# Pooled attention and a gated product: two batches' keys and values summed over eight by TensorE, conversions put behind the first product, and two more slots between a query's low part and its scores

## The chip, the cores and the metric

The kernel runs on one core of one Trainium2 chip. Its engines are TensorE (PE in the profile, with its weight loads as PEld), VectorE (DVE), ScalarE (ACT), GpSimd (POOL) and SyncE (SP), which here only starts DMAs. The metric is the device time of one execution in microseconds, as the median of several runs. The time before is 1088.79 us (three runs, 1088.64 to 1090.27).

## The reference

Queries, keys and values are [8 batches, 8 heads, 576 rows, 64]. Keys and values are averaged over groups of eight rows, so each head has 72 of them. Attention over these gives x with 4608 rows of 512. Then come two products with 1536 columns, their elementwise product, and a product back to 512 columns.

```python
k_p = k.reshape(B, H, Sp, pool, D).mean(axis=3)
v_p = v.reshape(B, H, Sp, pool, D).mean(axis=3)
scores = scale * np.matmul(q, k_p.transpose(0, 1, 3, 2))
scores = scores - np.max(scores, axis=-1, keepdims=True)
attn = np.exp(scores)
attn = attn / (np.sum(attn, axis=-1, keepdims=True) + 1e-09)
return np.matmul(attn, v_p).astype(np.float32)
...
a = x @ w_a
b = x @ w_b
return (a * b @ w_out).astype(np.float32)
```

The weights come from the host as 64-bit floating numbers (seen as pairs of 32-bit words), so the kernel has to convert them.

## The kernel before

**Precision.** Every matmul operand is split into a high part (a cast to float32r, by ScalarE) and a low part (the rest, a subtraction in the helper `low_part`, line 182, by VectorE or GpSimd). A product is then three matmuls: high by high, high by low and low by high. The names tell the part: `xh` and `xl`, `jha` and `jla` (weight a), `hh` and `hl` (gated product), `qh` and `ql` (queries).

**Tiles.** The 4608 rows make nine tiles of 512. A tile's products run over twelve column blocks f. `ffn_in(t, f)` makes `psa` and `psb` with 24 matmuls of 512 columns, and `gated` (line 551) multiplies them on VectorE. `ffn_out(t, f)` adds to four accumulators `acc` with 12 matmuls. A hand-written order takes tile 0 first. From block `LAG` = 4 on, tile 1 runs beside it, its gated product kept in DRAM and fetched later. From tile 2 on each tile runs alone.

**Attention.** The queries are cut into chunks of 128 or 64 rows; the first four (`early`) are all of tile 0 and belong to batch 0. Tile 1 takes the last 64 rows of batch 0 and most of batch 1. A chunk goes through `qh` (ScalarE), `ql` (GpSimd for the first four, else VectorE), scores on TensorE into `psc`, the maximum and its subtraction (lines 398 and 399 while i < `SUMMED`, else also a sum of two halves on line 434), the exponential, its sum and reciprocal, a multiplication (line 454), the split of the probabilities, transposes `ptr` (line 499), and per block of chunks the product with the values `po` (lines 532 to 535), whose parts are `xh` and `xl`. A tile's first product is issued only once the work of all its chunks has been (`have`, line 628).

**Keys and values.** `load_keys(b)` loads the four pairs of heads with 64 + 64 channels on the partitions. VectorE sums over eight (line 278). ScalarE and VectorE then write the high and low part to `kdiag`, which is block-diagonal over the two heads of a pair. `load_values(b)` does the same for `vdiag`. The values come from the host transposed, so that eight rows to be summed lie side by side. The last 8 of a head's 72 rows come from an extra array `vr`, three copies of them, and end in `vrem`. For batch 0 the raw data wait in parts of the weight buffers that aren't filled yet (`early_k` in `wb_raw`, `early_v` in `wo_raw`), and three of the four pairs of the values are summed by GpSimd in three additions (line 328). The two buffers of `kdiag` and `vdiag` alternate between batches.

**Weights.** `convert_weights(name, j, first)` goes through the twelve blocks of a, b and o. For each there are two ScalarE operations on the words (lines 222 and 223), three VectorE operations (224, 228 and 233) and the load of the next block's words. A block f + 1 is converted once product f - 1 of tile 0 has begun (`AHEAD` = 2, `begun`), so blocks 0 and 1 wait for no product. `split_weight` then makes the high and low parts for a product; the low part is on VectorE for a and b in the first twelve and on GpSimd otherwise.

**Order.** All engines' instructions are issued in an order that the class `Chains` works out at build time. Each piece of work is a generator. `yield n` lets n slots pass, `yield PE` queues for TensorE's turn, `wait` polls for marks, and ranks order what is due in one slot. `ffn_in` has four slots (one after every six wide matmuls), `ffn_out` two. Each engine then runs its instructions strictly in that order, held only by semaphores. Ahead of the first product `need` steps the chains until tile 0's x and the first parts of a and b are there. From tile 2 on, a chunk is started at `begin_at`, `CHUNK` = 32 slots ahead of its share of the previous tile's time, and loads of keys `KEYS_AHEAD` = 18 slots before that. After `ql`, `PROBS_GAP` = 2 slots pass before the scores; the same constant stands behind the probabilities. PSUM has one bank each for `psa` and `psb`, two for `att` (scores, transposes, `po`) and four for `acc`, which the first four chunks' scores borrow before the first product needs them.

Of the kernel before, what the change touches and what calls it, by code (L numbers as in the profile page):

```python
# [20 lines left out]
P = 128  # L21
# [27 lines left out]

SLOTS = 6  # L50
# [20 lines left out]
PROBS_GAP, VALUE_GAP = 2, 4  # L71
CHUNK = 32
# [4 lines left out]
EARLY_GAP, VALUES_START, KEYS_START, WEIGHTS_START, CONVERT_AFTER = 1, 2, 8, 10, 5  # L77


class Chains:  # L80
# [9 lines left out]
    def mark(self, *what):  # L90
        self.done.add(what)
# [30 lines left out]
def attn_moe_kernel(ctx: ExitStack, tc: tile.TileContext, q, k, v, vr, wa, wb, wo, out):  # L122
# [23 lines left out]
    mask = const.tile([P, 4], F32, name="mask")  # L146

# [38 lines left out]
    early_k = raw["b"].rearrange("p f c -> p (f c)")[:, NF * 512 - NK * S:].rearrange("p (g s) -> p g s", g=NK)  # L186
    early_v = raw["o"][:, NF - NK:, :]
    early_vr = raw["o"][:, NF - NK - NG:NF - NK, :]
# [5 lines left out]

    def load_early():
        load_raw_queries(0, early_q[:, 0])
        for g in range(NK):
            nc.sync.dma_start(early_k[:, g, :], k[0, :, g, :])
        load_raw_queries(1, early_q[:, 1])
        for g in range(0, NK, 2):  # L200
            nc.sync.dma_start(early_v[:, g:g + 2, :], v[0, :, g:g + 2, :])
        nc.sync.dma_start(early_vr[:NR], vr[0])
        for i in range(2, early):
            load_raw_queries(i, early_q[:, i])

    def convert_weights(name, j, first):
# [8 lines left out]
        yield first  # L215
        for f in range(NF):
            words = area[name].rearrange("p (c w) -> p c w", w=2)
# [19 lines left out]
            while f + 1 >= AHEAD and (len(begun) <= f + 1 - AHEAD or chains.now < begun[f + 1 - AHEAD] + 2 * j):  # L237
                yield 1
# [23 lines left out]

    def load_keys(b):
        kd = kdiag[b % 2]
        kp = tmp(f"kp_{b}")[:, :NK * SP].rearrange("p (g s) -> p g s", g=NK)
        for g0 in range(0, NK, 2):
            gs = slice(g0, g0 + 2)
            if b == 0:
                kraw = [early_k[:, g, :] for g in (g0, g0 + 1)]
            else:  # L270
                if g0:
                    yield from wait(("kraw", b, 0))
                kraw = [sb.tile([P, S], F32, tag="kv", name=f"kraw_{b}_{g}") for g in (g0, g0 + 1)]
                for j in range(2):
                    nc.sync.dma_start(kraw[j], k[b, :, g0 + j, :])
                yield 4
            for j in range(2):
# [6 lines left out]
                if b:  # L284
                    yield 1
            mark("kraw", b, g0)
            for e in range(2):
                r = slice(e * D, e * D + D)
                nc.scalar.mul(kd[r, gs, 0, e, :], kp[r, gs], 1.0 / POOL)
            if b:  # L290
                yield 1
            for e in range(2):
                r = slice(e * D, e * D + D)
                nc.vector.scalar_tensor_tensor(
                    out=kd[r, gs, 1, e, :],
                    in0=kp[r, gs],
                    scalar=1.0 / POOL,
                    in1=kd[r, gs, 0, e, :].bitcast(F32),
                    op0=ALU.mult,
                    op1=ALU.subtract,  # L300
                )
            mark("keys", b, g0)

    def load_values(b):
        vd = vdiag[b % 2]
        vrem = sb.tile([P, NG, 2, 2, D], F32R, tag="vrem", name=f"vrem_{b}")
        yield from wait(("keys", b, 2), ("values", b - 1))
        vp = sb.tile([P, NK + NG, D], F32, tag="vp", name=f"vp_{b}", bufs=1)
        for x0 in range(0, NK + NG, 2):
            if b == 0:  # L310
                vraw = [early_v[:, x, :] if x < NK else early_vr[:, x - NK, :] for x in (x0, x0 + 1)]
            else:
                if x0:
                    yield from wait(("vraw", b, x0 - 2))
# [463 lines left out]
```

## Time and profile before

| what | us |
|---|---|
| median of three runs | 1088.79 |
| the profiled execution | 1089.11 |
| its span | 1087.3 |
| outside the span | 1.8 |
| TensorE busy in the span | 1035.1 |
| VectorE busy | 589.7 |
| ScalarE busy | 515.3 |
| GpSimd busy | 513.0 |
| first product's first matmul starts | 70.19 |

The span runs from the first to the last instruction of the core. Busy times are sums over instructions. Those of TensorE are modelled at their ends, because matmuls overlap. A row of the timeline gives start, length, engine, line, operation, output and inputs, and in square brackets how long the engine stood idle before it and what released it. A row of the groups ends with busy time, mean length in nanoseconds, and idle time before. The mean granted TensorE clock of this execution is 0.993.

### The profile page before, as it was taken

To read this page: it belongs to the slowest core of one execution; us is meant where nothing else is said; L and a number is where in the kernel's file an instruction comes from. 1 tells how busy PE (TensorE), PEld (TensorE's weight loads), DVE (VectorE), ACT (ScalarE), POOL (GpSimd) and SP (SyncE) were. 2 spreads that over 40 slices of the span, in tenths; PEclk is the share of its full clock that TensorE was granted. 3 is DMA by queue.
4 is the path that set the end of the run, shared out by engine and by line. 5 is a ranking of instruction groups with operands and counts; after the bars stand their busy time and mean duration, and the time that the engine had idled before them with its cause. 6 is when DMAs were issued, how large, how long until landed. Compare 5 with 4: busy or idle time off the path is not lost.

```text
span 1087.3 us, 13572 instructions
## 1 busy us (share of the span) xinstructions
PE 1035.1 (95%) x4964; PEld 859.6 (79%) x4964; DVE 589.7 (54%) x941; ACT 515.3 (47%) x1035; POOL 513.0 (47%) x425
## 2 busy tenths in 40 slices
PE   4479999999999999999999999999998999999998
PEld 4367787888878888888877888888886888888886
DVE  8879967854675347534684346643567344322112
ACT  4656644454553454544553454444543454443332
POOL 6132200055565555555555555555554455554442
PEclk9999999999999999999999999999998999999999
DMA  6434445221330004000220002100220010001001
GB/s 219 117 129 135 141 136 174 93 94 46 114 109 1 1 23 127 26 1 1 95 90 1 1 19 90 45 1 1 93 83 0 1 59 1 1 1 39 1 1 39
DMA packets 32178, 63.79 MB, mean 59 GB/s; under 512 B 7376, under 2 KB 7376, under 8 KB 32112
## 3 DMA queue, kind: packets, MB, share of 16 engines
q1 hardware_dynamic: 32112, 62.93, 17.9%
q8 instruction: 39, 0.64, 0.2%
q14 instruction: 27, 0.22, 0.1%
HBM read 51.38 MB, written 11.53 MB: 58 GB/s over the span
## 4 chain that ended last, share of the span: by engine, by line
PE 84%; DVE 11%; ACT 2%; DMA 1%; issue 1%; SPq 0%; POOL 0%; DVEq 0%; ACTq 0%
PE psa L594 9%; PE psb L594 9%; PE acc L616 9%; PE psa L595 8%; PE psa L596 8%; PE acc L618 8%; PE acc L617 8%; PE psb L596 8%; PE psb L595 8%; PE ptr L499 2%; PE psc L428 2%; DVE ql L182 1%; DVE s L399 1%; PE psc L431 1%; PE po L534 1%
## 5 line engine op out<-in xcount | busy, mean ns | idle before, releaser
L551 DVE TENSOR_TENSOR h<-psb,h 128x512 f32<-128x512 f32 x108 | 74.5, 689 | 339.1 <-PE psb L596 335.0
L182 POOL TENSOR_TENSOR jlb<-wb_raw,jhb 128x512 fp32r<-128x512 f32 x88 | 114.5, 1301 | 264.1 <-ACT jhb L258 264.1
L182 POOL TENSOR_TENSOR jlo<-wo_raw,jho 128x512 fp32r<-128x512 f32 x108 | 144.0, 1334 | 116.5 <-ACT jho L258 116.5
L601 ACT COPY h<-psa 128x512 f32<-128x512 f32 x108 | 63.5, 588 | 268.6 <-PE psa L596 253.1
L594 PE MATMUL psa<-xh,jha 128*128 128x512 f32 x432 | 175.2, 406 | 0.0
L594 PE MATMUL psb<-xh,jhb 128*128 128x512 f32 x432 | 171.7, 398 | 0.6 <-DVE h L551 0.6
L616 PE MATMUL acc<-jho,hh 128*128 128x512 f32 x432 | 171.6, 397 | 0.0
L595 PE MATMUL psa<-xl,jha 128*128 128x512 f32 x432 | 170.8, 395 | 0.7 <-DVE xl L182 0.7
L596 PE MATMUL psa<-xh,jla 128*128 128x512 f32 x432 | 170.6, 395 | 0.0
L618 PE MATMUL acc<-jho,hl 128*128 128x512 f32 x432 | 168.6, 390 | 0.0
L596 PE MATMUL psb<-xh,jlb 128*128 128x512 f32 x432 | 168.6, 390 | 0.0
L595 PE MATMUL psb<-xl,jhb 128*128 128x512 f32 x432 | 168.5, 390 | 0.0
L617 PE MATMUL acc<-jlo,hh 128*128 128x512 f32 x432 | 168.3, 389 | 0.0
L182 POOL TENSOR_TENSOR jla<-wa_raw,jha 128x512 fp32r<-128x512 f32 x88 | 126.6, 1438 | 68.0 <-ACT jha L258 64.0
L564 ACT CAST hh<-h 128x512 fp32r<-128x512 f32 x100 | 62.2, 622 | 91.4 <-DVE h L551 86.7
L182 DVE TENSOR_TENSOR hl<-h,hh 128x512 fp32r<-128x512 f32 x100 | 90.2, 902 | 24.2 <-ACT hh L564 23.9
L596 PEld LDWEIGHTS psa<-xh,jla 128*128 128x128 f32 x432 | 82.6, 191 | 18.1
L595 PEld LDWEIGHTS psa<-xl,jha 128*128 128x128 f32 x432 | 82.8, 192 | 15.6 <-DVE xl L182 1.1
L618 PEld LDWEIGHTS acc<-jho,hl 128*128 128x128 f32 x432 | 81.1, 188 | 17.5
L596 PEld LDWEIGHTS psb<-xh,jlb 128*128 128x128 f32 x432 | 81.1, 188 | 17.4
L594 PEld LDWEIGHTS psa<-xh,jha 128*128 128x128 f32 x432 | 82.6, 191 | 15.0
L594 PEld LDWEIGHTS psb<-xh,jhb 128*128 128x128 f32 x432 | 81.2, 188 | 16.1 <-DVE h L551 1.0
(93 smaller groups left out, 1704.6 us busy)
## 6 DMA issues: line engine op xcount, KB each, us to landing
out<-y SPq DMA_DIRECT2D x36, 256.0 KB, 2.1
kraw<-in_k SPq DMA_DIRECT2D x28, 288.0 KB, 3.3
qraw<-in_q SPq DMA_DIRECT2D x28, 256.0 KB, 3.7
vraw<-in_v SPq DMA_DIRECT2D x28, 256.0 KB, 3.0
words<-in_wa SPq DMA_DIRECT2D x12, 512.0 KB, 3.5
words<-in_wb SPq DMA_DIRECT2D x12, 512.0 KB, 3.5
words<-in_wo SPq DMA_DIRECT2D x12, 512.0 KB, 3.6
vraw<-in_vr SPq DMA_DIRECT2D x14, 192.0 KB, 2.8
```

The costliest lines, as they stand in the source:

```text
L182: eng.tensor_tensor(out=lo, in0=src, in1=hi.bitcast(F32), op=ALU.subtract)
L428: nc.tensor.matmul(pt[:n, :2 * hk], qh[:, g, :n], kd[:, g].rearrange("p w e s -> p (w e s)"), start=True, stop=False)
L499: nc.tensor.transpose(ptr[:rows, g, :n], src, ident[:n, :n])
L551: nc.vector.tensor_tensor(out=h, in0=pt, in1=h, op=ALU.mult)
L564: nc.scalar.copy(hh, h)
L594: nc.tensor.matmul(pt, wh[:, c], xh[:, kk], start=(kk == 0), stop=False)
L595: nc.tensor.matmul(pt, wh[:, c], xl[:, kk], start=False, stop=False)
L596: nc.tensor.matmul(pt, wl[:, c], xh[:, kk], start=False, stop=(kk == NK - 1))
L601: nc.scalar.copy(h, pt)
L616: nc.tensor.matmul(acc[c], hh[:, cs], wh, start=first, stop=False)
L617: nc.tensor.matmul(acc[c], hh[:, cs], wl, start=False, stop=False)
L618: nc.tensor.matmul(acc[c], hl[:, cs], wh, start=False, stop=last)
```

## The change

Four things are done.

1. Keys and values of batches 0 and 1 come from the host in plain rows (`kn`, `vn`: 576 rows of 512 columns) and are loaded by `load_rows`, 128 rows to a partition block and 64 in the last, into unused parts of the weight buffers. TensorE sums over eight: `pool_keys` multiplies each block of the rows with `pool16`, a 128 x 16 matrix with a one where row and group agree, and gets keys already transposed; `pool_values` uses `place` and `remain`, which put each sum at its partition, in five matmuls that accumulate in `acc` banks. The splits, now in `split_keys` and `split_values`, read PSUM for these batches and SBUF for the others. The matmuls are in plain float32. `load_keys` and `load_values` stay for batches 2 to 7. The ranks and start slots of these chains change (`SPLITS` for batch 0, the rank behind the first four chunks for batch 1).
2. In `convert_weights` block 1 of a and b waits for the first product to begin, and o waits for the values of batch 1, whose raw data lie in its buffer, and for the first product. a's block 3 waits for the keys of batch 1.
3. `QUERY_GAP` = 4 slots stand between `ql` and the scores from tile 2 on (it was 2), and `CHUNK` is 34 (it was 32), so the scores keep their slot and `qraw`, `qh` and `ql` move ahead by two. Keys and values are tied to `begin_at` and move with it.
4. From tile 2 on a chunk's transposes wait until all weights are converted, since the transposed probabilities take the words' buffer.

```diff
+NB = -(-S // P)
+BY_PE = 2
...
-PROBS_GAP, VALUE_GAP = 2, 4
-CHUNK = 32
+QUERY_GAP, PROBS_GAP, VALUE_GAP = 4, 2, 4
+CHUNK = 34
...
+    pool16 = const.tile([P, P // POOL], F32, name="pool16")
+    words = raw["o"].rearrange("p f c -> p (f c)")
+    place = words[:, :NK * (P + P // POOL)].rearrange("p (k c) -> p k c", k=NK)
+    remain = words[:, 1024 - NR:1024]
...
+    early_k = [waiting("b", NF - NB), waiting("a", NF - early - NB)]
+    early_v = [waiting("o", NF - NB), waiting("o", NF - 2 * NB)]
...
+    def load_rows(dst, src):
+        whole = S // P
+        nc.sync.dma_start(dst[:, :whole], src[:whole * P].rearrange("(k p) c -> p k c", p=P))
+        nc.sync.dma_start(dst[:S - whole * P, whole], src[whole * P:])
...
     def load_early():
         load_raw_queries(0, early_q[:, 0])
-        for g in range(NK):
-            nc.sync.dma_start(early_k[:, g, :], k[0, :, g, :])
+        load_rows(early_k[0], kn[0])
         load_raw_queries(1, early_q[:, 1])
-        for g in range(0, NK, 2):
-            nc.sync.dma_start(early_v[:, g:g + 2, :], v[0, :, g:g + 2, :])
-        nc.sync.dma_start(early_vr[:NR], vr[0])
+        load_rows(early_v[0], vn[0])
...
         load_words(0)
         yield first
+        if name == "o":
+            yield from wait(("values", 1))
+            while not begun:
+                yield 1
         for f in range(NF):
+            if name == "a" and f == NF - early - NB:
+                yield from wait(("keys", 1, 2))
...
-            while f + 1 >= AHEAD and (len(begun) <= f + 1 - AHEAD or chains.now < begun[f + 1 - AHEAD] + 2 * j):
+            step = max(f + 1 - AHEAD, 0)
+            while len(begun) <= step or chains.now < begun[step] + 2 * j:
                 yield 1
...
+    def pool_keys(b):
+        if b:
+            load_rows(early_k[b], kn[b])
+            yield 4
+        yield PE
+        pt = ps.tile([P, 512], F32, tag="acc", name=f"pk_{b}", bufs=4)
+        for g in range(NK):
+            for blk in range(NB):
+                rows = rows_of(blk)
+                at = g * SP + blk * P // POOL
+                nc.tensor.matmul(
+                    pt[:, at:at + rows // POOL],
+                    early_k[b][:rows, blk, g * P:(g + 1) * P],
+                    pool16[:rows, :rows // POOL],
+                    start=True,
+                    stop=True,
+                )
+        kp = pt[:, :NK * SP].rearrange("p (g s) -> p g s", g=NK)
+        for g0 in range(0, NK, 2):
+            yield from split_keys(b, kp, g0)
...
+    def pool_values(b):
+        if b:
+            load_rows(early_v[b], vn[b])
+        yield from wait(("keys", b, 2), ("values", b - 1))
+        yield PE
+        pv = ps.tile([P, 512], F32, tag="acc", name=f"pv_{b}", bufs=4)
+        pr = ps.tile([P, 512], F32, tag="acc", name=f"pr_{b}", bufs=4)
+        flat_place = place.rearrange("p k c -> p (k c)")
+        for blk in range(NK):
+            nc.tensor.matmul(
+                pv, flat_place[:, blk * P:(blk + 1) * P], early_v[b][:, blk], start=(blk == 0), stop=(blk == NK - 1)
+            )
+        rows = rows_of(NK)
+        nc.tensor.matmul(pr[:NR], remain[:rows], early_v[b][:rows, NK], start=True, stop=True)
+        heads = pv.rearrange("p (g e d) -> p g e d", g=NK, e=2)
+        of_four = pr.rearrange("p (r c d) -> p r c d", r=NG, c=4)
+        yield from split_values(b, lambda r, e: heads[r, :, e], lambda r: of_four[:NR, r])
...
-        yield 1 if soon else PROBS_GAP
+        yield 1 if soon else QUERY_GAP
...
         yield from wait(("turned", i - 1), ("value", j - 1))
+        if t >= 2:
+            yield from wait(*(("weight", name, NF - 1) for name in ("a", "b", "o")))
...
         nc.vector.tensor_reduce(
+            out=pool16, in_=ident0.rearrange("p (k j) -> p k j", j=POOL), axis=AX.X, op=ALU.add
+        )
+        nc.gpsimd.memset(place, 0.0)
+        for e in range(2):
+            nc.gpsimd.tensor_copy(
+                place[:, :, e * KM:e * KM + P // POOL], pool16.unsqueeze(1).broadcast_to([P, NK, P // POOL])
+            )
+        nc.gpsimd.tensor_copy(
+            remain.rearrange("p (x s) -> p x s", s=KR), pool16[:, :KR].unsqueeze(1).broadcast_to([P, 3 * 4, KR])
+        )
...
-        chains.start(load_keys(0), KEYS)
+        chains.start(pool_keys(0), SPLITS)
...
-        chains.start(load_values(0), KEYS, VALUES_START)
-        chains.start(load_keys(1), KEYS, KEYS_START)
-        chains.start(load_values(1), KEYS, KEYS_START + 1)
+        chains.start(pool_values(0), SPLITS, VALUES_START)
+        chains.start(pool_keys(1), (CHUNKS[0], early), 8)
+        chains.start(pool_values(1), (CHUNKS[0], early), 8 + 1)
```

More of the change, by code (lines that the diff above doesn't have):

```diff
@@ L121, in attn_moe_kernel @@
 @with_exitstack
-def attn_moe_kernel(ctx: ExitStack, tc: tile.TileContext, q, k, v, vr, wa, wb, wo, out):
+def attn_moe_kernel(ctx: ExitStack, tc: tile.TileContext, q, k, v, vr, kn, vn, wa, wb, wo, out):
     nc = tc.nc
@@ L283, in load_keys @@
                 )
-                if b:
-                    yield 1
+                yield 1
             mark("kraw", b, g0)
[L287 to L301, printed above, removed]
@@ L302, in load_keys, with split_values @@
[L302 to L304 removed]
+            yield from split_keys(b, kp, g0)
+    def split_values(b, vp, vrp):
         vd = vdiag[b % 2]
         vrem = sb.tile([P, NG, 2, 2, D], F32R, tag="vrem", name=f"vrem_{b}")
[L307 to L314, printed above, removed]
[L315 to L332 removed]
@@ L333, in load_values @@
         for e in range(2):
             r = slice(e * KM, e * KM + KM)
[L335 removed]
+            nc.scalar.mul(vd[r, :, 0, r], vp(r, e), 1.0 / POOL)
         wide = tmp(f"vwide_{b}").rearrange("p (r j e d) -> p r (j e) d", r=NG, j=2, e=2)
@@ L366, in load_values @@
         mark("values", b)
+    def pool_values(b):
+        if b:
+            load_rows(early_v[b], vn[b])
[13 more added lines that the diff above has]
+        yield from split_values(b, lambda r, e: heads[r, :, e], lambda r: of_four[:NR, r])
+    def load_values(b):
+        yield from wait(("keys", b, 2), ("values", b - 1))
+        vp = sb.tile([P, NK + NG, D], F32, tag="vp", name=f"vp_{b}", bufs=1)
+        for x0 in range(0, NK + NG, 2):
+            if x0:
+                yield from wait(("vraw", b, x0 - 2))
+            vraw = [sb.tile([P, S], F32, tag="kv", name=f"vraw_{b}_{x0 + j}")[:, :D * POOL] for j in range(2)]
+            for j in range(2):
+                if x0 < NK:
+                    nc.sync.dma_start(vraw[j], v[b, :, x0 + j, :])
+                else:
+                    nc.sync.dma_start(vraw[j][:NR], vr[b, :, x0 + j - NK, :])
+            yield 3
+            for j in range(2):
+                x, rows = x0 + j, P if x0 < NK else NR
+                vv = vraw[j][:rows].rearrange("p (d j) -> p d j", j=POOL)
+                nc.vector.tensor_reduce(out=vp[:rows, x], in_=vv, axis=AX.X, op=ALU.add)
+            mark("vraw", b, x0)
+            yield 1
+        yield from split_values(
+            b,
+            lambda r, e: vp[r, :NK],
+            lambda r: vp[:NR, NK + r].unsqueeze(1).broadcast_to([NR, 4, D]),
+        )
     def chunk(i):
@@ L756 @@
     vrl = np.ascontiguousarray(np.repeat(vrl, 3, axis=1).reshape(B, NR, NG, D * POOL))
+    kn, vn = (
+        np.ascontiguousarray(x[:BY_PE].transpose(0, 2, 1, 3).reshape(BY_PE, S, DM)) for x in (k, v)
+    )
     wl = {
```

71 lines of the change are left out of this document (34 added, 37 removed).

## The prediction

> **What bounds the kernel now.** I read the page's totals first, then busy time by stretch with cuts at the first product, at the first product of tile 1 and round each pause of TensorE, then waits, groups and timeline.
>
> ```profile
> span 1087.3 us, 13572 instructions
> ...
> PE 1035.1 (95%) x4964; PEld 859.6 (79%) x4964; DVE 589.7 (54%) x941; ACT 515.3 (47%) x1035; POOL 513.0 (47%) x425
> ```
>
> ```profile
> 0.00:10.00 10.00, 1.91 (x7) 1.71 (x7) 5.99 (x10) 3.52 (x7) 5.79 (x11) 1.00 0.82 257
> 10.00:30.00 20.00, 13.15 (x63) 11.91 (x62) 18.70 (x36) 8.91 (x20) 13.94 (x18) 1.00 0.49 170
> 30.00:70.20 40.20, 19.65 (x97) 16.54 (x96) 30.36 (x58) 22.46 (x50) 10.01 (x11) 1.00 0.47 143
> 70.20:129.50 59.30, 55.76 (x278) 43.66 (x277) 55.86 (x93) 42.05 (x86) 16.33 (x13) 0.97 0.41 124
> ...
> 569.50:572.70 3.20, 0.00 (x1) 0.01 (x1) 3.20 (x2) 0.65 (x2) 3.20 (x4) 1.00 0.00 0
> 572.70:576.30 3.60, 3.60 (x12) 2.88 (x13) 1.40 (x3) 0.00 (x0) 1.81 (x2) 0.53 0.00 0
> ...
> 829.70:835.60 5.90, 5.87 (x18) 4.74 (x19) 3.44 (x7) 0.00 (x0) 1.83 (x2) 0.50 0.00 1
> 835.60:1087.30 251.70, 247.25 (x1167) 205.26 (x1165) 75.10 (x113) 99.90 (x192) 121.22 (x96) 0.99 0.04 15
> ```
>
> The columns are the stretch, its length, busy time of PE, PEld, DVE, ACT and POOL, the granted clock, DMA share and GB/s. TensorE is the bound as a whole: idle 1087.3 - 1035.1 = 52.2 us. Of that 70.2 - (1.91 + 13.15 + 19.65) = 35.5 us lie ahead of the first product and 3.5 us between it and tile 1. So little else is left that it can be named: two pauses of 3.2 us (the second ends at 829.7), each followed by a stretch at about half the clock.
>
> ```profile
> 70.19 0.79 PE L594 MATMUL psa<-xh,jha 128*128 128x512 f32 x1
> ...
> 129.77 0.50 PE L595 MATMUL psa<-xl,jha 128*128 128x512 f32 x1 [0.69 <-DVE xl L182]
> ```
>
> The first row is the first product, the second the first of tile 1, and what ends its wait is VectorE. From 10 to 30 us VectorE is busy 18.70 of 20 us, from 70.2 to 129.5 us 55.86 of 59.3. The start is therefore a queue of VectorE work: 5.99 + 18.70 + 30.36 + 55.86 = 110.9 us of it before 129.5 us, and 18.6 us without any. After 129.5 us it has room.
>
> The two pauses are these, in the list of TensorE's waits after 130 us and in the timeline of the first one:
>
> ```profile
> PE psc L431 <- DVE ql L182: 6.4, 2, 3.2
> ```
>
> ```profile
> 567.54 1.15 POOL L454 TENSOR_TENSOR s<-s,z 64x576 f32<-64x576 f32 x1 [4.76 <-ACT jho L258]
> 567.87 4.77 DVE L182 TENSOR_TENSOR ql<-qraw,qh 128x256 fp32r<-128x256 f32 x1
> 567.98 0.62 ACT L564 CAST hh<-h 128x512 fp32r<-128x512 f32 x1 [0.46 <-DVE h L551]
> 568.65 1.28 POOL L182 TENSOR_TENSOR jlb<-wb_raw,jhb 128x512 fp32r<-128x512 f32 x1
> 569.20 0.29 PE L428 MATMUL psc<-kdiag,qh 128*64 128x288 f32 x1
> 569.88 1.26 POOL L182 TENSOR_TENSOR jlo<-wo_raw,jho 128x512 fp32r<-128x512 f32 x1
> 571.10 1.25 POOL L182 TENSOR_TENSOR pr<-s,pr 64x512 fp32r<-64x512 f32 x1
> 572.57 0.80 DVE L182 TENSOR_TENSOR hl<-h,hh 128x512 fp32r<-128x512 f32 x1
> 572.70 0.28 PE L431 MATMUL psc<-kdiag,ql 128*64 128x144 f32 x1 [3.20 <-DVE ql L182]
> ```
>
> The subtraction that makes ql takes 4.77 us, though it has half of hl's elements and hl took 0.80. It stands beside four operations of GpSimd without a gap and ends with them. TensorE asks for ql at about 569.5 us. The second pause has the same shape and length 257 us later.
>
> **The change, part by part.** (a) *Sums over eight on TensorE.* For batches 0 and 1 these groups of VectorE before 129.5 us, and these of GpSimd before 70 us, go:
>
> ```profile
> L278 DVE TENSOR_REDUCE kp<-kraw 128x72 f32<-128x576 f32 x4 | 2.9, 732 | 0.0
> L278 DVE TENSOR_REDUCE kp<-wb_raw 128x72 f32<-128x576 f32 x4 | 2.9, 750 | 0.8 <-DMA wb_raw<-in_k 0.7
> L330 DVE TENSOR_REDUCE vp<-vraw 128x64 f32<-128x512 f32 x4 | 2.5, 674 | 0.0
> L671 DVE TENSOR_REDUCE mask<-ident 96x4 f32<-96x96 f32 x1 | 1.8, 1792 | 0.0
> L330 DVE TENSOR_REDUCE vp<-vraw 96x64 f32<-96x512 f32 x2 | 1.3, 674 | 0.0
> L330 DVE TENSOR_REDUCE vp<-wo_raw 96x64 f32<-96x512 f32 x2 | 1.3, 672 | 0.0
> L330 DVE TENSOR_REDUCE vp<-wo_raw 128x64 f32<-128x512 f32 x1 | 0.7, 687 | 0.0
> ```
>
> ```profile
> L328 POOL TENSOR_TENSOR wo_raw<-wo_raw 128x256 f32<-128x256 f32 x3 | 2.2, 727 | 0.0
> L328 POOL TENSOR_TENSOR wo_raw<-wo_raw 128x128 f32<-128x128 f32 x3 | 1.2, 401 | 0.2
> ```
>
> VectorE loses 2.9 + 2.9 + 2.5 + 1.3 + 1.3 + 0.7 = 11.6 us and GpSimd 2.2 + 1.2 us and three smaller additions. VectorE gains one reduction for the pooling matrix, at most the 1.8 us of the mask's; I take 1.0, which lies ahead of the keys' arrival. GpSimd gains a memset and three small copies in the same place. So 110.9 becomes 100.3 us of VectorE work before tile 1: 10.6 us less. The splits of keys and values now read PSUM; I cost that at nothing, since the subtractions of scores that read PSUM take no longer than their size asks.
>
> TensorE gains per batch 20 matmuls for the keys (four groups by five row blocks, 16 columns each) and 5 of 512 columns for the values, all in float32. No row shows such a matmul. The nearest are the short ones of the scores, and the products at half clock after the first pause:
>
> ```profile
> 9.69 3.14 PE psc L414 x12
> ```
>
> ```profile
> 573.65 0.63 PE L595 MATMUL psa<-xl,jha 128*128 128x512 f32 x1
> ...
> 574.08 0.63 PE L596 MATMUL psa<-xh,jla 128*128 128x512 f32 x1
> ```
>
> That is 3.14 / 12 = 0.26 us for a short one and 574.08 - 573.65 = 0.43 us between wide ones. By these a batch costs 20 x 0.26 + 5 x 0.43 = 7.4 us. From above I bound each by the 0.79 us of the first product's first matmul, 25 x 0.79 = 20 us a batch; from below by 0.1 us each, 2.5 us. I take 7.4, two batches 15 us, nearest in shape. It lies in TensorE's 35.5 idle us; without that cover it would be paid in full.
>
> What it costs VectorE is waiting. These rows are the start of the kernel, and the first conversion:
>
> ```profile
> 6.49 0.67 ACT L289 ACTIVATE kdiag<-kp 64x144 fp32r<-64x144 f32 x2 [2.48 <-DVE kp L278]
> ...
> 7.52 1.41 DVE L278 TENSOR_REDUCE kp<-wb_raw 128x72 f32<-128x576 f32 x2
> ...
> 10.61 0.45 DVE L398 TENSOR_REDUCE m<-psc 128x4 f32<-128x288 f32 x1
> ```
>
> ```profile
> 35.27 0.68 ACT L222 ACTIVATE wa_raw<-words 128x512 f32<-128x512 f32 x1
> ...
> 48.52 0.68 DVE L228 SCALAR_TENSOR_TENSOR wo_raw<-words,wo_raw 128x512 int32<-128x512 int32 x1
> ```
>
> Before, the first scores ran when half of the keys was reduced; now all of kn must land, about 7.5 us (the last two key reductions start then), and 20 matmuls run first: 7.5 + 5.2 + 0.7 (ScalarE's pair of splits) + 0.9 (half the scores of a chunk before the maximum) makes 14.3 us for the first maximum, where it was 10.6. VectorE then idles some 4 us more at the start. The values' matmuls and batch 1's stand in TensorE's queue among transposes and scores that the first product needs, and hold three of the four acc buffers; I give that 2.6 us of new idle time. The loads move too: kn and vn of both batches (1.18 MB each) go ahead of the first words, but a0's conversion started at 35.3 us, long after they land.
>
> Start: -10.6 + 4 + 2.6 = **-4.0 us**, between -10.6 (no new idle) and +12 (below).
>
> (b) *Conversions behind the first product.* a1, b1, o0 and o1 no longer stand ahead of it; each costs VectorE three operations of about 0.6 us (one is quoted above). They aren't saved: some 7 us move from the stretch 30 to 70.2, where VectorE idles 9.8 us and TensorE 20.5, to the one after, where VectorE is at 94%. The first product comes sooner, perhaps at 60 us, and the second then waits for a1. What counts is when tile 1 begins, and until then VectorE has the same total. I cost (b) at 0, between -4 (the shorter chain to the first product takes idle time from VectorE) and +4 (pauses after which TensorE runs at half clock).
>
> (c) *Four slots from ql to the scores*, with every chunk begun two slots sooner. A slot is six wide matmuls; the last stretch above has 251.7 / 1167 = 0.216 us for one, so 1.3 us a slot, and two make 2.6. ql is then asked for 1.6 + 2.6 = 4.2 us before TensorE needs it, and at that place GpSimd waits 4.76 us for work just before its train. Each pause is worth its 3.2 us and half of the slow stretch: 3.6 / 2 = 1.8 and 5.9 / 2 = 2.9. Together 3.2 + 1.8 + 3.2 + 2.9 = 11.1 us. The loads of keys and values move two slots as well, past nothing that waits. Because hl comes next in VectorE's queue and meets the same train, I take **-9 us** of it, between -3.1 and -11.1.
>
> (d) *The wait of tile 2's turned probabilities for the last weights.*
>
> ```profile
> L233 DVE CUSTOM_DVE_ANT_0 wo_raw<-wo_raw,wlow_o x12: 691/693/695, 49.2 to 200.8; 128x1024 uint16<-128x1024 uint16 x12
> ```
>
> The last conversion is at 200.8 us, and the probabilities take the words' own buffer, of which there is one: they have to come behind it already. Without that cover it would delay tile 2's scores behind it by as much as the conversions slip. Cost 0.
>
> Sum: 1089.1 (the profiled execution: span 1087.3 and 1.8 around it; the median shown is 1088.8) - 4 - 9 = **1076 us**.
>
> By the Trainium skill, FP8 and Floating Point Precision, TensorE Precision Notes, true FP32 takes four passes through the array, which speaks against (a). By it a batch would cost four times 7.4, some 30 us at this clock, an estimate; no row here shows it.
>
> **The rivals.** *The wait passes to hl.* hl's high part is ready at 568.60 us, in the train. If it waits as ql did, to about 572.2 (ql's end, 572.64, less half of 0.80), the score reductions behind it free no PSUM before some 573.3 us, and the scores' second half, due near 571.1 us (569.2, half a us of their own and a slot), waits 2.2 us, with 1.8 at half clock: 4.0 twice is 8.0, so only 3.1 us are won: 1089.1 - 4 - 3.1 = 1082. For: the same two SBUF inputs as ql. Against: hl took 0.80 us when it came behind the train. The Trainium skill, SBUF, Who interferes with whom, lets the second of two such operations wait for the one in front only; by it hl would lose about 1 us and this rival fell, but the 4.77 us across four operations disagrees.
>
> *VectorE's relief goes through*: TensorE's additions hide fully and the shorter chain takes 4 more: 1089.1 - 10.6 - 4 - 9 = 1066. For: TensorE is idle half of the first 70 us. Against: the acc buffers and the keys' longer chain.
>
> *The pooling becomes the bound of the start* (slower). TensorE can do none of it before 7.5 us, and has 34.7 us of other work before the first product. At t us for each of 50 matmuls the product cannot come before 7.5 + 34.7 + 50 t; that passes 70.2 from t = 0.56, and eats the 9 us of (c) from t = 0.74. At the bound of 0.79 it is 81.7: +11.5 - 9 = 1091.6, about 1092. For: nothing shows a float32 matmul, several passes would carry t there, and short bursts run at half clock. Against: the keys' have 16 columns where the scores' have 144. The skill's four passes, named above, are what would bring it.
>
> *The change doesn't do what it says*: other stalls of ql's kind appear elsewhere, as every chunk moves two slots, and the start gains nothing: 1088.
>
> **How the numbers follow.** Forecast about 1076: 0.41. Passed to hl, 1082: 0.21. Full relief, 1066: 0.15. Nothing won, 1088: 0.10. Slower, 1092: 0.13. A measurement of this kernel can tell 0.2%, some 2.2 us, from no change. The first three cases are faster: 0.77. The fourth is within: 0.10. The last is slower: 0.13. The range goes from 1065, below the full relief, to 1089, above the case of no gain; it leaves out the slower case and the extremes of (a) and (b).
>
> **What would show it.** Right: no VectorE reduction of kp or vp for batches 0 and 1; the first score maximum at 13 to 16 us; the first product at 55 to 65 us and tile 1's at 120 to 128; no wait of psc for ql over 1 us after 130 us; 250 us of the later stretch without a half clock. Wrong: pooling matmuls above 0.56 us; PEclk near 0.5 in places where it was 1.00; hl above 3 us with psc waiting for the reductions behind it; a first product before 60 us with tile 1 no sooner than 129.

## The result, and the profile after

| | before | after |
|---|---|---|
| median, us | 1088.72 (1088.12 to 1090.27) | 1103.48 (1101.36 to 1105.18) |
| profiled span, us | 1087.3 | 1101.3 |

Four runs each; the ratio is 1.0133, with an interval of 1.0121 to 1.0144. The change makes the kernel 14.8 us slower where 13 us faster was forecast, and 1103.5 lies above the forecast's range, which ended at 1089.

The first lines of the page of the changed kernel, to be held against the page's first rows of before:

```profile
span 1101.3 us, 13757 instructions
...
PE 1058.1 (96%) x5064; PEld 873.4 (79%) x5064; DVE 573.4 (52%) x925; ACT 515.7 (47%) x1035; POOL 503.3 (46%) x420
```

VectorE has 16 us less to do (573.4 against 589.7), TensorE 23 us more (1058.1 against 1035.1), with 100 more instructions. The same kernel's busy time by stretch, cut at both ends of the two poolings, and then ahead of tile 1 as a whole; columns as in the prediction's:

```profile
7.66:24.45 16.79, 16.79 (x50) 11.85 (x51) 1.22 (x4) 2.51 (x7) 1.27 (x1) 1.00 1.02 339
24.45:39.44 14.99, 10.40 (x63) 9.78 (x63) 12.77 (x28) 6.57 (x14) 7.32 (x7) 0.67 0.00 0
39.44:56.06 16.62, 16.62 (x59) 12.26 (x58) 5.61 (x13) 7.02 (x19) 4.42 (x5) 0.58 0.00 1
...
0.00:145.40 145.40, 115.75 (x541) 90.94 (x541) 98.48 (x179) 76.84 (x162) 42.41 (x47) 0.84 0.42 128
```

In the first and third stretch TensorE never stops, and VectorE has 1.22 of 16.79 and 5.61 of 16.62 us to do. That is the pooling: TensorE runs in order, so all that the others wait for stands behind it. (The trace's records of the granted clock begin at 22.67 us in this run and at 74.52 in the kernel before; a row ahead of that prints 1.00 without a record.) The timeline of the changed kernel, cut to the pooling, to what VectorE waited for, and to the first rows of the first product and of tile 1:

```profile
7.63 9.34 PEld L316 LDWEIGHTS pk<-pool,wb_raw 128*128 128x128 f32 x40 [7.63 <-issue]
7.66 9.40 PE L316 MATMUL pk<-pool,wb_raw 128*128 128x16 f32 x40 [7.66 <-DMA wb_raw<-in_kn]
...
16.99 6.50 PE L395 MATMUL pv<-wo_raw 128*128 128x512 f32 x8
...
17.78 0.62 DVE L296 SCALAR_TENSOR_TENSOR kdiag<-pk,kdiag 64x144 fp32r<-64x144 f32 x2 [12.13 <-ACT kdiag L291]
...
23.43 1.10 PE L399 MATMUL pr<-wo_raw 64*96 64x512 f32 x2
...
24.56 0.75 DVE L357 SCALAR_TENSOR_TENSOR vwide<-pr,mask 96x256 f32<-96x256 f32 x2 [4.88 <-PE pr L399]
...
25.38 0.46 DVE L459 TENSOR_REDUCE m<-psc 128x4 f32<-128x288 f32 x1
...
39.44 9.39 PE L316 MATMUL pk<-pool,wa_raw 128*128 128x16 f32 x40
...
49.49 0.63 DVE L296 SCALAR_TENSOR_TENSOR kdiag<-pk,kdiag 64x144 fp32r<-64x144 f32 x2 [6.23 <-ACT kdiag L291]
49.52 5.58 PE L395 MATMUL pv<-wo_raw 128*128 128x512 f32 x8
...
79.32 0.79 PE L657 MATMUL psa<-xh,jha 128*128 128x512 f32 x1
...
145.70 0.50 PE L658 MATMUL psa<-xl,jha 128*128 128x512 f32 x1 [0.67 <-DVE xl L191]
```

A float32 matmul shows as two instructions: x40 are the 20 of the keys, x8 the four of the values. So one of 16 columns takes 9.40 / 20 = 0.47 us and one of 512 columns 6.50 / 4 = 1.6 us (the second batch's 5.58 / 4 = 1.4). The loads of the keys as stationary operand (PEld) run through 9.34 of the 9.40 us: by these rows the short matmuls last as long as their loads, and their few columns don't make them cheap. The first batch takes 16.8 us, from 7.66 to 24.45. The second takes 15.9, its 16.62 without 0.75 of transposes that lie in it. Both take 33 us, where the forecast had 15. The brackets show who pays: VectorE idles 12.13, 4.88 and 6.23 us, 23 in three places. The first maximum comes at 25.4 us, not 14.3.

The place of the first old pause, in the timeline of the changed kernel:

```profile
588.40 1.29 POOL L191 TENSOR_TENSOR jlb<-wb_raw,jhb 128x512 fp32r<-128x512 f32 x1
588.87 3.85 DVE L191 TENSOR_TENSOR hl<-h,hh 128x512 fp32r<-128x512 f32 x1 [0.69 <-ACT hh L627]
589.65 1.29 POOL L191 TENSOR_TENSOR jlo<-wo_raw,jho 128x512 fp32r<-128x512 f32 x1
590.90 1.27 POOL L191 TENSOR_TENSOR pr<-s,pr 64x512 fp32r<-64x512 f32 x1
592.14 0.76 POOL L191 TENSOR_TENSOR rem<-s,rem 64x64 fp32r<-64x64 f32 x1
592.64 1.76 DVE L495 TENSOR_REDUCE s<-psc 64x144 f32<-64x288 f32 x4
593.14 0.35 PE L489 MATMUL psc<-kdiag,qh 128*64 128x288 f32 x1 [1.14 <-DVE s L495]
```

ql is no longer late: no wait of psc for ql is left after 130 us. hl stands in the same train of GpSimd work instead, for 3.85 us, and the reduction behind it frees the scores' bank too late: TensorE waits 1.14 us. It has waited 1.43 us at 581.17 already, for another reduction of the scores; where that wait comes from, gap_only shows below.

**Where the 14.8 us arise.** All kernels below make the same 108 products in the same order. The table gives when ScalarE's copy of `psa` of the n-th of them starts (the copy that writes `h`; n = 6 is tile 1's first, 25 tile 2's first), less the same time of the kernel before. Each column is one profiled execution.

| n (before, us) | after | after_ahead | one_pass | one_pass_free | defer_only | defer_begun | gap_only | gap_keys | gap_mult |
|---|---|---|---|---|---|---|---|---|---|
| 1 (75.58) | +9.3 | +12.0 | -9.6 | -2.6 | -8.0 | -9.0 | +0.7 | +0.3 | +0.6 |
| 3 (100.67) | +15.9 | +17.6 | -2.5 | -5.5 | +8.4 | -2.5 | +0.7 | +0.3 | +0.6 |
| 6 (132.29) | +15.9 | +17.2 | -2.5 | -6.5 | +9.1 | -2.5 | +0.7 | +0.3 | +0.7 |
| 16 (203.38) | +15.1 | +16.3 | -3.4 | -7.4 | +7.3 | -2.9 | +0.4 | +0.3 | +0.7 |
| 19 (223.29) | +18.1 | +19.5 | -0.2 | -4.0 | +7.3 | -2.9 | +3.5 | +0.3 | +3.8 |
| 51 (545.78) | +19.0 | +22.7 | +1.5 | -3.0 | +7.4 | -2.8 | +4.6 | +0.4 | +4.2 |
| 54 (578.02) | +17.4 | +21.1 | -0.1 | -4.6 | +8.4 | -2.8 | +3.0 | -1.7 | +1.0 |
| 78 (802.82) | +17.2 | +21.0 | -0.2 | -4.8 | +8.5 | -2.8 | +2.4 | -2.3 | +0.4 |
| 81 (836.22) | +14.4 | +18.2 | -3.0 | -7.6 | +7.4 | -4.1 | -0.4 | -4.1 | -3.9 |
| 108 (1074.72) | +14.5 | +18.4 | -2.9 | -7.4 | +7.3 | -4.1 | -0.4 | -4.1 | -4.0 |

The changed kernel loses 9.3 us ahead of the first product, 6.6 more by the third, and 3.0 between the 16th and the 19th. At the two old pauses it wins (between 51 and 54 it goes from +19.0 to +17.4, between 78 and 81 from +17.2 to +14.4). The start costs 15.9, not -4. (c) wins 1.6 + 2.8 at the pauses and gives back 3.0.

### The profile page after: what moved, and what is told of

Its sections match the earlier page's. It is cut to its first block, busy times and chain, and to the rows that moved or that the text cites. A ratio compares the mean times of both kernels' runs of the same rounds, so it can differ in the third digit from the quotient of the medians.

```text
span 1101.3 us, 13757 instructions
## 1 busy us (share of the span) xinstructions
PE 1058.1 (96%) x5064; PEld 873.4 (79%) x5064; DVE 573.4 (52%) x925; ACT 515.7 (47%) x1035; POOL 503.3 (46%) x420
## 4 chain that ended last, share of the span: by engine, by line
PE 86%; DVE 7%; ACT 3%; DMA 2%; issue 2%; POOL 0%; SPq 0%; DVEq 0%; ACTq 0%; POOLq 0%
PE psb L657 8%; PE psa L657 8%; PE acc L679 8%; PE psb L659 8%; PE psb L658 8%; PE psa L658 8%; PE psa L659 8%; PE acc L681 8%; PE acc L680 8%; PE ptr L560 2%; PE pk L316 2%; PE psc L489 2%; PE pv L395 1%; PE psc L475 1%; PE po L598 1%
## 5 line engine op out<-in xcount | busy, mean ns | idle before, releaser
L191 POOL TENSOR_TENSOR jla<-wa_raw,jha 128x512 fp32r<-128x512 f32 x88 | 120.8, 1372 | 74.2 <-ACT jha L281 66.9
L191 DVE TENSOR_TENSOR hl<-h,hh 128x512 fp32r<-128x512 f32 x100 | 92.8, 928 | 33.6 <-ACT hh L627 33.4
L659 PEld LDWEIGHTS psa<-xh,jla 128*128 128x128 f32 x432 | 81.8, 189 | 18.4 <-DVE jla L191 0.8
L681 PEld LDWEIGHTS acc<-jho,hl 128*128 128x128 f32 x432 | 81.1, 188 | 17.4
```

The lines of the kernel that those rows point to most:

```text
L191: eng.tensor_tensor(out=lo, in0=src, in1=hi.bitcast(F32), op=ALU.subtract)
L659: nc.tensor.matmul(pt, wl[:, c], xh[:, kk], start=False, stop=(kk == NK - 1))
L681: nc.tensor.matmul(acc[c], hl[:, cs], wh, start=False, stop=last)
```

## The experiments

Two readings of the start stood against each other: that the float32 matmuls hold TensorE, or that the conversions moved behind the first product are what comes late. For the rest the question was why four slots bring so little.

**after_ahead: the changed kernel with block 1 of a and b converted ahead again.**

```diff
-            step = max(f + 1 - AHEAD, 0)
-            while len(begun) <= step or chains.now < begun[step] + 2 * j:
+            while f + 1 >= AHEAD and (len(begun) <= f + 1 - AHEAD or chains.now < begun[f + 1 - AHEAD] + 2 * j):
```

> The changed kernel with block 1 of a and b converted ahead of the first product again; o stays behind. Theory D2 (the deferred conversions cost the 6.6 us between first and third product): first product 2 to 4 us later, third product 2 to 5 us sooner, time 1098 to 1101. Theory P: what is put ahead fills VectorE's idle time while TensorE pools, so nothing is lost at the first product and up to 6 us is won after it: 1097 to 1099. Rival: no change, 1102 to 1105.

1105.91 us, ratio 1.0151 [1.0136, 1.0166]. Tile 1 begins 1.2 us later than in the changed kernel, and the time lies above all three that were expected. Putting the conversions of a and b back ahead of the first product wins nothing, so they are not what makes this start late.

**one_pass: the changed kernel with its pooling in one pass.** The matmuls read only the upper half of each word, as bfloat16, so keys and values of the two batches are shortened.

```diff
+    def upper(ap):
+        return ap.bitcast(BF16)[:, 1::2]
...
-                    early_k[b][:rows, blk, g * P:(g + 1) * P],
-                    pool16[:rows, :rows // POOL],
+                    upper(early_k[b][:rows, blk, g * P:(g + 1) * P]),
+                    upper(pool16[:rows, :rows // POOL]),
```

(the values' matmuls likewise)

> The changed kernel with its pooling matmuls on the upper halves of the words as bfloat16, so each is one pass; the sums are of shortened keys and values. Theory P (the float32 matmuls' length, 9.4 + 7.5 us a batch, is what makes the start late): they take a quarter or less, the first scores come 11 to 13 us sooner, tile 1 starts 12 to 20 us sooner than 145, time 1083 to 1092. Rival W (waiting for all of the keys, the acc banks and the order of the pieces make it late): tile 1 sooner by less than 6 us, time 1097 to 1102.

1085.7 us, ratio 0.9966 [0.9955, 0.9978]. The timeline of this kernel, for batch 1's pooling, the first maximum, and the first rows of the first product and of tile 1:

```profile
15.58 0.46 DVE L463 TENSOR_REDUCE m<-psc 128x4 f32<-128x288 f32 x1 [0.73 <-PE psc L479]
...
29.64 1.41 PE L320 MATMUL pk<-pool,wa_raw 128*128 128x16 bf16 x20
...
31.94 1.93 PE L399 MATMUL pv<-wo_raw 128*128 128x512 bf16 x4
33.80 0.66 PE L403 MATMUL pr<-wo_raw 64*96 64x512 bf16 x1
...
60.93 0.79 PE L661 MATMUL psa<-xh,jha 128*128 128x512 f32 x1
...
127.30 0.50 PE L662 MATMUL psa<-xl,jha 128*128 128x512 f32 x1 [0.69 <-DVE xl L192]
```

The 20 matmuls of the keys take 1.41 us against 9.39, four of the values 1.93 against 5.58. Nothing else in the program differs, and tile 1 comes at 127.30, 18.4 us sooner. (The first maximum comes 9.8 us sooner, a little less than expected.) The first maximum at 15.58, the first product at 60.93 and tile 1 at 127.30 lie inside the windows that the prediction named (13 to 16, 55 to 65, 120 to 128). The length of the float32 matmuls is the loss at the start, and a cheaper pass is all it takes to turn the sign.

**late_values: the changed kernel with batch 0's values summed behind the second chunk's scores** (one run).

```diff
-        yield from wait(("keys", b, 2), ("values", b - 1))
+        yield from wait(("keys", b, 2), ("values", b - 1), ("scores", 1))
```

> The changed kernel with the matmuls of batch 0's values behind the second chunk's scores instead of ahead of the first's. Theory Q (the queue's order counts, the first scores wait for values that nothing needs yet): first maximum at 18 to 19 us instead of 25.4, first product 3 to 7 us sooner than 79.4, span 1094 to 1098. Rival S (the sum of TensorE's float32 work counts, wherever it stands): first product within 2 us of 79.4, span 1099 to 1103.

1103.56 us; row 6 of the table would read +16.1 for it. The first maximum comes 5.2 us sooner, at 20.15 us, the first product only 1.2, and tile 1 no sooner. So the place of these matmuls in TensorE's queue makes no difference to tile 1, as the rival S had it.

**one_batch: the changed kernel with batch 1 summed the old way** (one run).

```diff
-        chains.start(pool_keys(1), (CHUNKS[0], early), 8)
-        chains.start(pool_values(1), (CHUNKS[0], early), 8 + 1)
+        chains.start(load_keys(1), KEYS, 8)
+        chains.start(load_values(1), KEYS, 8 + 1)
```

> The changed kernel with batch 1's keys and values loaded and summed in the old way (VectorE), batch 0's still on TensorE. Theory P: batch 1's float32 matmuls stand for 16 us in TensorE's queue amid tile 0's transposes, so without them the first product comes 8 to 14 us sooner than 79.4 and tile 1 starts 6 to 12 us sooner than 145; span 1090 to 1096. Rival B0 (batch 0's 17 us ahead of the first scores are what counts, batch 1's lie in idle time): tile 1 sooner by less than 3 us or later, span 1099 or more.

1113.65 us, far from both expectations. The copy of the first product comes 7.8 us sooner than in the changed kernel, but by the third product the kernel is at +20.9. o's first conversion starts at 100.9 us here and at 80.4 in the changed kernel. The next run has the same turn.

**defer_only: the kernel before with (b) alone, with o's wait for the values of batch 1.** (d) comes with it, as in all kernels with (b).

```diff
+        if name == "o":
+            yield from wait(("values", 1))
+            while not begun:
+                yield 1
...
-            while f + 1 >= AHEAD and (len(begun) <= f + 1 - AHEAD or chains.now < begun[f + 1 - AHEAD] + 2 * j):
+            step = max(f + 1 - AHEAD, 0)
+            while len(begun) <= step or chains.now < begun[step] + 2 * j:
```

> The kernel before with the conversions of block 1 of a and b, and of all of o, put behind the first product, and with tile 2's wait for the weights. Theory D (the deferral costs what it gives): the first product comes 5 to 10 us sooner, the next two come closer to where they were, tile 1 starts within 3 us of 129.5; time 1086 to 1093. Rival D2 (the deferral alone loses the 6.6 us that the changed kernel loses between its first and third product): tile 1 later by 4 to 7 us, time 1093 to 1096. Rival D3 (the shorter start goes through): 1080 to 1084.

1095.13 us, 1.0056 [1.0043, 1.0069], in the range of rival D2, though for another reason, as defer_begun will show. The first product is 8.0 us sooner, the third 8.4 later. With the old sums batch 1's values come late, and o's blocks wait for them. The timeline of this kernel, for o's first conversion and what waits for it:

```profile
90.20 0.65 ACT L226 ACTIVATE wo_raw<-words 128x512 f32<-128x512 f32 x1
...
96.89 0.62 ACT L263 CAST jho<-wo_raw 128x512 fp32r<-128x512 f32 x1 [3.15 <-DVE wo_raw L237]
...
97.56 0.79 PE L623 MATMUL acc<-jho,hh 128*128 128x512 f32 x1 [2.09 <-ACT jho L263]
```

So this run and one_batch measured a wait that the changed kernel doesn't have in this form, and neither can price (b).

**defer_begun: (b) alone, o waiting only for the first product.**

```diff
         if name == "o":
-            yield from wait(("values", 1))
             while not begun:
                 yield 1
```

(against defer_only)

> The kernel before with the deferral as in the earlier run, but o waits for the first product only and not for the values of batch 1, which here come late. Theory V (the 7.6 us that the deferral lost came from o's wait for these values): tile 1 starts within 3 us of 129.5, time 1085 to 1091. Rival D2 (block 1 of a and b being late loses it): tile 1 later by 4 us or more, time 1093 to 1096.

1086.91 us, 0.9974 [0.996, 0.9988], as theory V had it: what defer_only lost was o's wait. The first product comes 9.0 us sooner, and 6.4 of them are paid back by the third. The waits of TensorE from the first product to the third's copy (engine, line, what it waited for, us, times, longest), in the kernel before, in defer_begun and in the changed kernel, the longest one of each:

```profile
PE ptr L499 <- DVE xl L182: 1.6, 1, 1.6
```

```profile
PE ptr L503 <- DVE xl L182: 4.6, 1, 4.6
```

```profile
PE ptr L560 <- DVE xl L191: 4.6, 1, 4.6
```

The same transposes, waiting in TensorE's queue for xl from VectorE, stand 4.6 us where they stood 1.6, with the moved conversions now in VectorE's queue. What remains of (b) is -2.5 at tile 1.

**one_pass_free: one_pass with a's and b's blocks 1 ahead again, and o waiting for batch 1's values only.** The keys and values are shortened as in one_pass.

```diff
             yield from wait(("values", 1))
-            while not begun:
-                yield 1
...
-            step = max(f + 1 - AHEAD, 0)
-            while len(begun) <= step or chains.now < begun[step] + 2 * j:
+            while f + 1 >= AHEAD and (len(begun) <= f + 1 - AHEAD or chains.now < begun[f + 1 - AHEAD] + 2 * j):
```

> The changed kernel with one-pass pooling (shortened keys and values), block 1 of a and b converted ahead of the first product, and o waiting for batch 1's values only. Theory D2 (deferral costs): tile 1 sooner by 2 to 5 us than with one-pass pooling alone, time 1080 to 1084. Rival (what is put ahead of the first product delays it by as much, as in the changed kernel): 1085 to 1089.

1083.38 us, 0.995 [0.9934, 0.9966]. The first product is 7 us later than in one_pass and tile 1 is 4.0 sooner: -6.5. Once the sums cost little, VectorE is free early: in one_pass it idles 20.8 us ahead of the first product and 7.9 between it and tile 1, so work moved behind the first product is moved into the fuller stretch.

**gap_only: the kernel before with (c) alone.**

```diff
-PROBS_GAP, VALUE_GAP = 2, 4
-CHUNK = 32
+QUERY_GAP, PROBS_GAP, VALUE_GAP = 4, 2, 4
+CHUNK = 34
...
-        yield 1 if soon else PROBS_GAP
+        yield 1 if soon else QUERY_GAP
```

> The kernel before with four slots between ql and the scores and CHUNK 34, and nothing else of the change. Theory H (the wait is handed on): ql leaves GpSimd's train, hl takes its place in it (3 to 4 us long) and the score reductions behind hl hold TensorE about 1.1 us per pause without a half clock, so of the 11.1 us about 4 to 5 are won and the time is 1083 to 1086. Rival F (the slots remove the pauses): 1077 to 1079. Rival N (the changed kernel's new waits of 1.4 us before each pause come from these slots): 1086 to 1088.

1087.88 us, 0.999 [0.9979, 1.0001]: nothing that can be told from no change, the time of rival N. The waits of TensorE after 130 us in this kernel:

```profile
PE psc L428 <- DVE s L434: 7.1, 6, 1.5
PE ptr L499 <- DVE s L434: 1.9, 1, 1.9
```

The two waits of 3.2 us are gone; six smaller ones have come, for the scores' reductions instead of ql. The timeline of this kernel at tile 2's first chunks, where before had no wait, and ahead of the first old pause:

```profile
209.53 1.49 DVE L330 TENSOR_REDUCE vp<-vraw 96x64 f32<-96x512 f32 x2 [2.21 <-DMA vraw<-in_vr]
...
212.69 0.81 DVE L434 TENSOR_REDUCE s<-psc 128x144 f32<-128x288 f32 x2
213.19 0.40 PE L428 MATMUL psc<-kdiag,qh 128*128 128x288 f32 x1 [1.54 <-DVE s L434]
...
559.52 1.34 DVE L330 TENSOR_REDUCE vp<-vraw 96x64 f32<-96x512 f32 x2 [2.15 <-DMA vraw<-in_vr]
...
566.77 0.34 PE L428 MATMUL psc<-kdiag,qh 128*64 128x288 f32 x1 [1.41 <-DVE s L434]
```

The values' sums moved ahead by two slots with everything else. In VectorE's queue they now stand ahead of the scores' reductions and wait 2.21 us for a transfer that hasn't landed. That is the +3 between products 16 and 19. The same happens ahead of each old pause: at the first VectorE waits 2.15 us for the transfer and TensorE 1.41 us behind it. The wait of 1.13 us behind hl comes 12 us later, at 578.74, so each old place has two waits with different causes.

**gap_keys: gap_only with the loads and sums of keys and values back in their place.**

```diff
-KEYS_AHEAD, VALUES_AFTER = 18, 16
+KEYS_AHEAD, VALUES_AFTER = 16, 16
```

> The kernel before with four slots from ql to the scores and CHUNK 34 as in gap_only, but KEYS_AHEAD 16, so loads, reductions and splits of keys and values keep their old slots. Theory N (gap_only's new waits of TensorE for score reductions come from the moved reductions of values, which stand ahead of them in VectorE's queue and wait for DMA): those waits fall from 9 us to under 4, tile 2 starts within 1 us of before, time 1082 to 1085. Rival (they come from ql and hl): waits as in gap_only, 1087 to 1089.

1085.31 us, 0.9971 [0.9959, 0.9982]. The +3 is gone (+0.3 in row 19), and so are the waits of 1.41 us ahead of the old pauses. But two waits of 2.5 us are left, at the old places, where under 4 us in all had been expected: the wait behind hl has grown from 1.13 us. The timeline of this kernel at the first:

```profile
569.40 4.30 DVE L182 TENSOR_TENSOR hl<-h,hh 128x512 fp32r<-128x512 f32 x1 [0.69 <-ACT hh L564]
573.62 1.76 DVE L434 TENSOR_REDUCE s<-psc 64x144 f32<-64x288 f32 x4
574.11 0.35 PE L428 MATMUL psc<-kdiag,qh 128*64 128x288 f32 x1 [2.50 <-DVE s L434]
```

This is the rival of hl alone: it priced the wait at 2.2 us, and it is 2.50. Its half clock came behind the second of the two waits (2.48 us) and not behind the first, where the row to 577.50 prints 1.00:

```profile
828.47:832.30 3.83, 3.83 (x14) 2.60 (x14) 2.71 (x5) 0.15 (x1) 0.99 (x1) 0.55 0.01 2
```

What (c) wins at the two pauses in this run is 2.1 + 1.8 us.

**gap_mult: gap_only with the first link of that train moved.** The multiplication of the probabilities of 64-row chunks goes to VectorE.

```diff
-        (nc.vector if first and i % 2 else nc.gpsimd).tensor_tensor(
+        (nc.vector if (first and i % 2) or (not soon and n < P) else nc.gpsimd).tensor_tensor(
```

> gap_only with the multiplication by the reciprocal of the 64-row chunks from tile 2 on done by VectorE instead of GpSimd. Theory H (hl is held by GpSimd's train that this multiplication starts): hl under 2 us at the two places, no wait of 1.1 us for score reductions there, some 2 us less than gap_only, 1084 to 1087. Rival: VectorE's added 0.75 us delays the reductions as much, 1087 to 1089.

1085.0 us, 0.9969 [0.9957, 0.9982]. At the old place hl takes 0.68 us in the timeline of this kernel:

```profile
574.78 0.68 DVE L182 TENSOR_TENSOR hl<-h,hh 128x512 fp32r<-128x512 f32 x1
```

The +3 at tile 2's start stays, and so do the waits of 1.41 us ahead of the old pauses, as gap_keys's cure isn't in it. The two runs cure different waits at the same places.

**best_old_sums: the kernel before with (b) as in defer_begun, (c), and both cures.** Sums stay on VectorE, and nothing is shortened. **best_one_pass: one_pass_free with both cures**, keys and values shortened as there. Their edits are those shown.

> The kernel before, its sums over eight as they were, with the conversions of block 1 of a and b and all of o behind the first product (o waits for nothing else), four slots from ql to the scores, KEYS_AHEAD 16, and the 64-row chunks' multiplication on VectorE. If the parts add up: 2.5 us at the start from the deferral, 4 from the slots with keys and values left in place, 3 to 5 from hl no longer held: 1077 to 1081. Rival (the parts meet in VectorE's queue): 1082 to 1086.

> one_pass_free (sums on TensorE in one pass of shortened words, block 1 of a and b ahead, o behind batch 1's values) with KEYS_AHEAD 16 and the 64-row chunks' multiplication on VectorE. If the parts add up: 6.5 us at the start, 4 from keys and values left in place, 3 to 5 from hl: 1073 to 1078. Rival: 1079 to 1083.

1074.89 us, 0.9878 [0.9862, 0.9894], and 1072.48, 0.9864 [0.9846, 0.9883], both a little below what was expected from adding up the parts. The waits of TensorE from 140 us to the end in best_old_sums:

```profile
PE ptr L503 <- DVE s L438: 1.7, 1, 1.7
PE psb L600 <- DVE h L557: 0.2, 1, 0.2
```

No wait of the scores is left. 1088.43 (the kernel before, beside these two) less 1074.89 is 13.5 us. It is near what the forecast put the pauses at, 11.1, with defer_begun's 2.5: 13.6. By the copies of `psa`, as in the table, 1.8 us of it are won by tile 1, 4.8 and 6.0 across the two old pauses (the forecast's 5.0 and 6.1), and the rest in small steps between. That this is more than the single runs add up to fits the two waits at one place: with only the one for the transfer cured, the one behind hl grew. The median of best_one_pass is 2.4 us lower still, but the two intervals overlap, and it sums shortened keys and values.

## Why the prediction was wrong, point by point

**The relief of VectorE: right.** VectorE has 98.48 us of work ahead of tile 1, where it had 110.9: 12.4 less, forecast 10.6.

**The price of the pooling on TensorE: the step that failed.** It said "By these a batch costs 20 x 0.26 + 5 x 0.43 = 7.4 us" and took it "nearest in shape". The rows were of float32r matmuls; a plain float32 one is two instructions and takes 0.47 us (keys) or 1.4 to 1.6 (values), and a batch is 16.8 and 15.9. The bounds (2.5 to 20) held it, the value taken was less than half. The argument that the keys' have only 16 columns failed too, as their time goes into the loads of the keys. VectorE's idle time ahead of tile 1 shows the cost:

| ahead of tile 1, us | VectorE busy | idle | tile 1 begins |
|---|---|---|---|
| before | 110.9 | 18.6 | 129.5 |
| forecast (-4) | 100.3 | 25.2 | 125.5 |
| one_pass | 98.6 | 28.7 | 127.3 |
| after | 98.5 | 46.9 | 145.4 |

The forecast's 4 + 2.6 of new idle time is 10.1 in one_pass, where the pooling is cheap, and 28.3 in the changed kernel. The 18.2 between the last two are the float32 matmuls' doing, shown by one edit. By the Trainium skill, FP8 and Floating Point Precision, TensorE Precision Notes, true FP32 takes four passes. The trace agrees for the wide ones. In the changed kernel the loads of the second batch's values, one to an instruction, start 0.85 us apart at a granted clock of 0.50, and 0.43 apart once it is 1.00, from 53.39 us on:

```profile
51.34 0.34 PEld L395 LDWEIGHTS pv<-wo_raw 128*128 128x128 f32 x1 [0.52 <-issue]
52.19 0.34 PEld L395 LDWEIGHTS pv<-wo_raw 128*128 128x128 f32 x1 [0.52 <-issue]
...
53.65 0.19 PEld L395 LDWEIGHTS pv<-wo_raw 128*128 128x128 f32 x1 [0.27 <-issue]
54.08 0.19 PEld L395 LDWEIGHTS pv<-wo_raw 128*128 128x128 f32 x1 [0.24 <-issue]
```

Two instructions make 1.7 us a matmul at half clock, four times the 0.43 that the prediction quotes for a wide float32r one, at half clock too. Over the whole second batch the rows add up to 9.39 + 5.58 + 1.10 = 16.1 us, against 1.41 + 1.93 + 0.66 = 4.0 in bfloat16, also four times, though the keys' part is 6.7. The prediction named the four passes and gave their mechanism 0.13. Its 30 us a batch came out too high by the keys: 4 x 20 x 0.26 = 20.8 us where 9.4 were measured, while 4 x 5 x 0.43 = 8.6 is near the first batch's 7.5 (from 16.99 to 24.45).

**The slower rival: its mechanism is what happened, its size was short.** It said that the product cannot come before 7.5 + 34.7 + 50 t and that t decides from 0.56 and 0.74. Measured, t = 33 / 50 = 0.66, which gives 75.2; the first product came at 79.32. The rival stopped there. By the third product 6.6 us more are lost, and the busy times of the two kernels over the stretch from the first product's first matmul to the third's copy show how:

```profile
70.19:100.70 30.51, 28.15 (x139) 22.26 (x139) 28.20 (x49) 20.77 (x44) 6.03 (x5) 0.94 0.38 117
```

```profile
79.32:116.60 37.28, 29.15 (x139) 22.24 (x138) 30.60 (x52) 24.73 (x49) 6.57 (x5) 0.84 0.49 140
```

The same 139 matmuls; TensorE's idle time grows from 2.4 to 8.1 us, and its busy time by 1.0 at a lower granted clock (the kernel before has no clock record for the first 4 us of its stretch). defer_begun and one_pass lose 6.4 and 7.1 us there, with a like wait for xl (4.6 and 4.9 us). But after_ahead, without the deferral of a and b, loses 5.6 too, by other waits of transposes and scores for VectorE and ScalarE. So the moved conversions alone don't explain it in the changed kernel, and what share they have stays open. The sum closes to within half a us: 79.3 - 70.2 = 9.1, and 6.6, less (c)'s 1.4, on 1089.1 make 1103.4.

**(b) at 0: inside its bounds.** It is -2.5 with the old sums. That the first product comes sooner and tile 1 hardly does was foreseen ("the second then waits for a1"); what TensorE then waits for longest is xl from VectorE; that the conversions ahead of it make it late is argued, not shown. In one_pass against one_pass_free, (b)'s delays cost 4.0. Its price depends on where VectorE has room.

**(c) at -9: wrong, -1.4.** Two steps failed. "I take -9 us of it": the rival in which the wait passes to hl was right, 1.1 to 2.5 us a place. And "The loads of keys and values move two slots as well, past nothing that waits": VectorE's sums move with them, wait for their transfer and hold the scores' reductions, +3.0 at tile 2's start and 1.4 us ahead of each old pause. Of the pauses' worth, 11.1 us, nearly all is there to be had: with both causes removed best_old_sums wins 10.8 there. The rival's half clock did not come behind the changed kernel's waits of 1.1 and 1.4 us; in gap_keys it came behind one of two of 2.5.

**(d) at 0: right.** defer_begun has (d), and stands at -2.9 both at product 16 and at 19, round the start of tile 2's chunks.

**The signs.** Of those named for being wrong, two came: the pooling matmuls above 0.56 us (0.66 on average) and hl above 3 us with psc waiting for the reductions behind it. The sign of PEclk can't be read for the first 74.5 us, because the 1.00 in the prediction's first rows stands for no record.

## What to carry to other kernels

Before work is moved to an idle engine, price it in the operand type it will really have: a row of the same shape in another type is not near. Look at the loads of its stationary operand as well as at its columns. An engine that runs in order and has idle time only because others haven't fed it doesn't have that time to give: what is put there delays the very work that would feed the others. And where a whole group of steps is moved to relieve one wait, ask of each what it now stands ahead of in its engine's queue.

## What the runs showed of the hardware

- A matmul in plain float32 is recorded as two instructions. With 512 columns it took 1.7 us at a granted clock of 0.50 and 0.86 at 1.00 (the steps of 0.85 and 0.43 us above). The keys' 20 took 9.39 us at 0.50, nearly all of it loads of the stationary operand, and 9.40 ahead of the trace's first clock record.
- The granted clock of 1.00 in a row ahead of the first record is not a measurement. In the kernel before, with its first record at 74.52 us, the wide matmuls of the first products start 0.43 us apart up to 74.39 and 0.23 apart from 74.69, so they ran at about half clock up to there.
- hl, a VectorE subtraction of two SBUF inputs, took 0.68 us in gap_mult, where GpSimd had no work beside it, 3.85 in the changed kernel, held across three GpSimd operations without a gap, and 4.30 in gap_keys. By the Trainium skill, SBUF, Who interferes with whom, it would have waited for the one in front only; as with ql's 4.77 us before, these rows disagree.
- Both pauses of TensorE of 3.2 us were followed by a half clock in the kernel before. In gap_keys one of two of 2.5 us was. After the one of 1.14 us (the changed kernel, stretch from its end) none came:

```profile
593.14:597.00 3.86, 3.86 (x20) 2.87 (x20) 2.62 (x5) 1.43 (x3) 1.00 (x1) 1.00 0.00 0
```
